# Plain-head v loads of five later batches issued from ScalarE's queue instead of SyncE's, in a fused sliding-attention and gated-unit kernel

## Chip, cores, metric

The kernel runs on one core of one Trainium2 chip. The metric is the device time in microseconds of one execution; lower is better. Three executions of the kernel before gave 179.93, 181.99 and 182.55 us, a median of 181.99 us. The profile shown below is of an execution of 178.74 us, in which the instructions span 176.8 us.

## What is computed

Eight batches, eight heads, 576 positions, head width 64. Heads 0 to 3 ("plain") attend to the last 32 positions, heads 4 to 7 ("dilated") to every fourth of the last 128. The attention output, 512 wide, goes through a gated linear unit with a causal convolution over five positions:

```python
scores = (q @ k^T) / 8, masked: plain  0 <= rel < 32;  dilated  0 <= rel < 128 and rel % 4 == 0
attn   = softmax(scores);  x = concat_heads(attn @ v)        # [8, 576, 512]
gate   = sigmoid(sum_k conv_w[k] * x shifted by 4 - k)
out    = (gate * (x @ w_val)) @ w_out                        # float32
```

All inputs and the output are float32 in main memory. The arithmetic on TensorE is bfloat16.

## The kernel before

The work is cut into 16 groups: group `g` is batch `g // 2`, with the plain heads where `g` is even and the dilated heads where it is odd. A group has two pairs of heads, and each pair is one step `i`, so there are 32 steps, four to a batch. A step computes scores (`scores`, L438), exponentials on ScalarE (L469), masks on VectorE (L478), the product with v (`attn_v`, L480) and the normalization (L517). In the same step stand, for earlier pairs, the convolution and its gate (`conv`, L569; the gate is ScalarE's L603), one to three value products (`val`, L606, each closed by L617 on VectorE), and output tiles (`out_tile`, L623: TensorE L628, ScalarE's copy `osb` L633, then one or two stores from L639). The next group is transposed meanwhile (`trans_main` L361 and `trans_rest` L408).

The order on each engine is the order in which the program states it: the kernel turns the scheduler off with `manual_schedule`, and the main loop (L734 to L803) writes out what each step holds. An engine takes its own instructions in that order.

Loads run three groups ahead. At the first pair of a group the loop calls `load_group(g + 3)` (L748), which issues the main parts of k and q (L122), the last 64 positions of k and q (`qk_rest`, L137 for plain groups and L142 for dilated ones), and then v. For a dilated group v is `v_st` and `vB_st` (L174 and L177). For a plain group v is two DMAs of L157, one for each half of the partitions of `vPst`, 64 partitions x 12 x 128 elements, 384 KB each; rows overlap between blocks, so 768 KB are moved. There are two `vPst` buffers, taken in turn by batches. `prep_v` (L197) casts them on GpSimd to the bfloat16 tile `vP`.

All these loads and all output stores are issued by SyncE, whose queue holds them in program order: at the beginning of a step it has k, q, rests and v of a later group, and at the end of a step the stores of a finished output tile. A store waits for ScalarE's `osb`. Only three small DMAs at the start go out from ScalarE. Every DMA adds 16 to one of eight completion semaphores, which SyncE's and ScalarE's DMAs share, and before it is issued its queue waits until the DMA that had that semaphore last has landed. So at most eight DMAs are under way at once, from both queues together. These eight are called lanes below[...].

Of the kernel before, what the change touches and what calls it, by code (L numbers as in the profile page):

```python
# [23 lines left out]
def kernel(  # L24
# [11 lines left out]
    nc = tc.nc  # L36
# [80 lines left out]
    def load_main(g, name, a, e, eng):  # L117
        src, h0 = (q if name == "q" else k), 4 * (g % 2)
        t = grp_tiles.setdefault(g, {})
        if name not in t:  # L120
            t[name] = qk_pool.tile([128, 4, DIL * D], FP32, name=f"{name}_nat")
        eng.dma_start(  # L122
            out=t[name][:, a:e, :],
            in_=src[g // 2, h0 + a:h0 + e, 0:RM, :].rearrange("h (p r) d -> p h (r d)", r=DIL))

    def load_rest(g, name, eng):


        src = k if name == "k" else q
        b, dil = g // 2, g % 2  # L130
        t = grp_tiles.setdefault(g, {})
        if "rest" not in t:
            t["rest"] = qk_pool.tile([128, 2, 2 * D], FP32, name="qk_rest")
        dst = t["rest"][:, 0 if name == "k" else 1, :]
        off = src.offset + ((b * H + 4 * dil) * S + RM) * D
        if not dil:
            eng.dma_start(  # L137
                out=dst.rearrange("p (h d) -> p h d", h=2),
                in_=bass.AP(tensor=src.tensor, offset=off,
                            ap=[[D, S - RM], [2 * S * D, 2], [S * D, 2], [1, D]]))  # L140
        else:
            eng.dma_start(  # L142
                out=dst,
                in_=bass.AP(tensor=src.tensor, offset=off,
                            ap=[[2 * D, 2 * TR], [S * D, 4], [1, 2 * D]]))

    def load_v_half(g, z, a, e, eng):


        b, per = g // 2, NB // 2  # L150
        first, dst = a * per, vPst[b % NVP]
        if b == 0 and a == 0 and z == 0:
            eng.dma_start(
                out=dst[16:D, 0, :],
                in_=v[0, 0, 0:96, :].rearrange("(p j) d -> p (j d)", j=2))
            first = 1
        eng.dma_start(  # L157
            out=dst[D * z:D * z + D, first:e * per, :],
            in_=bass.AP(
                tensor=v.tensor,  # L160
                offset=v.offset + (b * H * S + 192 * first + 96 * z - 32) * D,
                ap=[[2 * D, D], [192 * D, e * per - first], [1, 2 * D]]))

    def load_v(g, a=0, e=4, eng=nc.sync):
        b, dil = g // 2, g % 2
        t = grp_tiles.setdefault(g, {})
        if not dil:
            for z in range(2):
                load_v_half(g, z, a, e, eng)
        else:  # L170
            if "vst" not in t:
                t["vst"] = vst_pool.tile([128, 4, DIL * D], FP32, name="v_st")
                t["vBst"] = vst_pool.tile([128, 4, 2, D], FP32, name="vB_st")
            eng.dma_start(  # L174
                out=t["vst"][:, a:e, :],
                in_=v[b, 4 + a:4 + e, 0:RM, :].rearrange("h (p r) d -> p h (r d)", r=DIL))
            eng.dma_start(  # L177
                out=t["vBst"][:, a:e].rearrange("p h j d -> p h (j d)"),
                in_=v[b, 4 + a:4 + e, DIL * TB:S, :].rearrange("h (p j) d -> p h (j d)", j=2))

    def load_group(g):
        for name in ("k", "q"):
            load_main(g, name, 0, 4, nc.sync)
        for name in ("k", "q"):
            load_rest(g, name, nc.sync)
        load_v(g)

    def cast(g, name):

# [23 lines left out]
    def pair_info(i):  # L213
        b, c = i // NCH, i % NCH
        dil = int(c >= NCH // 2)
        return b, c, dil, 2 * b + dil, (c % 2) * 2
# [517 lines left out]
    for i in range(NP):  # L734
        b, c, dil, g, a = pair_info(i)

        if i == 0:
            load_weight(0, moe_w_val)
            load_pair(2, 0)
        elif i == 1:  # L740
            load_pair(2, 2)
        elif i == 2:
            load_weight(1, moe_w_out)
            load_pair(3, 0)
        elif i == 3:
            load_pair(3, 2)
            load_group(4)
        if c % 2 == 0 and 5 <= g + 3 < 2 * B:  # L748
            load_group(g + 3)
# [93 lines left out]
```

The softmax here doesn't subtract the row's maximum and nothing guards it: scores larger than these inputs give would overflow.

## Time and profile before

| | |
|---|---|
| device time, median of three | 181.99 us (179.93 to 182.55) |
| TensorE matmul busy | 159.5 us, 90% of the span |
| VectorE busy | 119.5 us, 68% |
| ScalarE busy | 113.8 us, 64% |
| GpSimd busy | 64.5 us, 36% |
| DMA traffic | 43.43 MB, 246 GB/s over the span |
| DMAs of L157 from SyncE, issue | 20 issues, 602 / 618 / 1896 ns (min, median, max) |
| DMAs of L157, issue to landing | 4.0 / 7.6 / 9.2 us |

A page of the profile has the busy time of each engine, the span cut in 40 slices with the busy share of each in tenths, the chain of work that ended last, the groups of instructions with their mean durations, and the DMA issues. "SPq" and "ACTq" are the issue queues of SyncE and ScalarE; the duration of an entry there is the time in which the queue is taken up by the DMA, the wait for its lane often included, and not the transfer. A timeline lists an engine's instructions in order of time: start, duration, engine, line, operation, and in square brackets how long the engine was idle before and what released it.

### The profile page before, as it was taken

The page shows a single profiled execution, that of the slowest core. Times are in us where ns is not written, and L with a number is a line of the kernel's source. Part 1 is how long each engine was busy: PE and PEld are TensorE (multiplying, and loading weights), DVE is VectorE, ACT ScalarE, POOL GpSimd, SP SyncE. Part 2 cuts the span into 40 slices and gives each one's busy share as a digit, 9 for nine tenths or more (in the row PEclk, how much of TensorE's full clock was granted, in tenths as well). Part 3 has the DMA queues.
Part 4 walks back from the last instruction along what each step waited for, and adds up shares of the span by engine and source line. Part 5 has one row for each costly group of instructions (what it writes and reads, how often), then busy time and mean ns, then how long its engine had stood idle before and what let it go on. Part 6 is the DMA issues. An engine that isn't in the chain of part 4 may idle for free.

```text
span 176.8 us, 6900 instructions
## 1 busy us (share of the span) xinstructions
PE 159.5 (90%) x2875; PEld 106.6 (60%) x2875; DVE 119.5 (68%) x299; ACT 113.8 (64%) x215; POOL 64.5 (36%) x129
## 2 busy tenths in 40 slices
PE   6798877989898899999997999789999999999990
PEld 2355544666576676677665667557677766665540
DVE  4397849773768776888695677577697869783320
ACT  3437835558777577778776777378867886654441
POOL 7673449659407610770085009300940500000000
PEclk9969999999999999999999999999999999999998
DMA  4999999999999999999999999999999322224344
GB/s 148 240 268 348 325 230 285 324 303 237 296 335 243 318 335 343 173 287 356 307 188 300 345 318 192 330 323 329 204 360 339 112 63 59 63 63 120 102 159 155
DMA packets 51528, 43.43 MB, mean 246 GB/s; under 512 B 6965, under 2 KB 45861, under 8 KB 51498
## 3 DMA queue, kind: packets, MB, share of 16 engines
q1 hardware_dynamic: 50944, 42.67, 89.1%
q8 instruction: 22, 0.36, 0.9%
q10 hardware_dynamic: 554, 0.34, 0.6%
q14 instruction: 8, 0.07, 0.1%
HBM read 33.56 MB, written 9.44 MB: 243 GB/s over the span
## 4 chain that ended last, share of the span: by engine, by line
PE 63%; DMA 21%; ACT 6%; DVE 5%; issue 2%; SPq 1%; ACTq 0%
PE ps_bank L628 16%; PE ps_bank L611 15%; PE ps_bank L594 10%; DMA out_dram<-osb 8%; PE ps_bank L378 5%; DMA qk_rest<-in_q_dram 4%; DMA k_nat<-in_k_dram 3%; DMA vPst<-in_v_dram 3%; PE ps_sc L499 3%; PE ps_sc L513 3%; PE ps_sc L449 3%; PE ps_bank L548 2%; DMA q_nat<-in_q_dram 2%; PE ps_sc L466 2%; DVE et L478 2%
## 5 line engine op out<-in xcount | busy, mean ns | idle before, releaser
L469 ACT ACTIVATE et<-ps_sc 128x576 bf16<-128x576 f32 x64 | 38.2, 649 | 13.7 <-PE ps_sc L449 9.0
L633 ACT ACTIVATE osb<-ps_bank 128x512 f32<-128x512 f32 x36 | 21.9, 609 | 28.9 <-PE ps_bank L628 18.0
L617 DVE SCALAR_TENSOR_TENSOR y<-gate,ps_bank 128x288 bf16<-128x288 bf16 x64 | 28.3, 450 | 13.0 <-PE ps_bank L611 10.6
L594 PE MATMUL ps_bank<-xT,conv_diag 64*64 64x288 bf16 (+1 forms) x768 | 27.6, 266 | 0.6 <-ACT osb L633 0.6
L529 DVE TENSOR_TENSOR xn<-ps_sc,rec 128x768 bf16<-128x768 f32 (+1 forms) x27 | 25.8, 955 | 0.9
L603 ACT ACTIVATE gate<-ps_bank 128x288 bf16<-128x288 f32 x64 | 23.1, 423 | 1.8 <-PE ps_bank L594 1.7
L478 DVE TENSOR_TENSOR et<-et,mask_d 128x576 bf16<-128x576 bf16 x32 | 15.8, 495 | 10.2 <-ACT et L469 10.2
L611 PE MATMUL ps_bank<-xT,w_val_s 128*128 128x288 bf16 x128 | 20.7, 285 | 2.1 <-issue 1.3
L193 POOL CAST k_b<-k_nat 128x512 bf16<-128x512 f32 x10 | 6.5, 681 | 42.3 <-DMA k_nat<-in_k_dram 33.1
L594 PEld LDWEIGHTS <-conv_diag 64*64 64x64 bf16 x768 | 18.9, 106 | 3.6 <-issue 1.2
L611 PE MATMUL ps_bank<-xT,w_val_b 128*128 128x288 bf16 x128 | 20.1, 286 | 0.4 <-DVE xT L563 0.4
L628 PEld LDWEIGHTS <-y 128*128 128x128 bf16 x144 | 12.6, 97 | 11.8 <-DVE y L617 0.9
L478 DVE TENSOR_TENSOR et<-et,mask_p 128x576 bf16<-128x576 bf16 x32 | 16.0, 501 | 4.8 <-ACT et L469 4.8
L202 POOL CAST vP<-vPst 128x768 bf16<-128x768 f32 x16 | 13.1, 841 | 15.6 <-DMA vPst<-in_v_dram 5.8
L628 PE MATMUL ps_bank<-w_out_s,y 128*128 128x512 bf16 x72 | 18.3, 379 | 0.1
L628 PE MATMUL ps_bank<-w_out_b,y 128*128 128x512 bf16 x72 | 18.5, 379 | 0.0
L563 DVE COPY xT<-ps_bank 128x576 bf16<-128x576 bf16 x32 | 14.6, 455 | 4.7 <-PE ps_bank L561 2.4
L611 PEld LDWEIGHTS <-w_val_s 128*128 128x128 bf16 x128 | 12.0, 97 | 6.2 <-issue 1.0
L207 POOL CAST vA<-v_st 128x512 bf16<-128x512 f32 x16 | 11.3, 705 | 10.3 <-DMA v_st<-in_v_dram 5.3
L611 PEld LDWEIGHTS <-w_val_b 128*128 128x128 bf16 x128 | 11.6, 98 | 3.7 <-issue 0.2
L393 ACT COPY kT<-ps_bank 128x1024 bf16<-128x1024 bf16 (+1 forms) x10 | 8.5, 849 | 6.1 <-PE ps_bank L370 5.9
L528 DVE RECIPROCAL rec<-ps_sc 128x12 f32<-128x12 f32 (+1 forms) x27 | 6.2, 231 | 7.7 <-PE ps_sc L499 6.7
(100 smaller groups left out, 248.4 us busy)
## 6 DMA issues: line engine op xcount, KB each, us to landing
k_nat<-in_k_dram SPq DMA_DIRECT2D x12, 512.0 KB, 6.0
q_nat<-in_q_dram SPq DMA_DIRECT2D x12, 512.0 KB, 6.9
vPst<-in_v_dram SPq DMA_DIRECT2D x12, 384.0 KB, 7.7
v_st<-in_v_dram SPq DMA_DIRECT2D x6, 512.0 KB, 5.7
k_nat<-in_k_dram SPq DMA_DIRECT2D x8, 256.0 KB, 5.9
out_dram<-osb SPq DMA_DIRECT2D x8, 256.0 KB, 6.1
q_nat<-in_q_dram SPq DMA_DIRECT2D x7, 256.0 KB, 5.8
out_dram<-osb SPq DMA_DIRECT2D x8, 224.0 KB, 5.4
```

Of the source, the lines that this page charges most:

```text
L202: nc.gpsimd.tensor_copy(vPs[b % NVP][:, a:e, :, 0:D], vPst[b % NVP][:, a * NB // 2:e * NB // 2, :].rearrange("p (h u) (j d) -> p h (u j) d ...
L207: nc.gpsimd.tensor_copy(vAs[b % NVD][:, a:e, :, 0:D], t["vst"][:, a:e, :].rearrange("p h (r d) -> p h r d", r=DIL))
L469: nc.scalar.activation(out=e3, in_=ps[:, :, 0:HB], func=AF.Exp, scale=scale)
L478: nc.vector.tensor_tensor(out=e3, in0=e3, in1=m, op=ALU.mult)
L529: nc.vector.tensor_tensor(out=dst, in0=av[:, :, :, 0:D], in1=rec[0:R, :, :, None].to_broadcast([R, 2, 6, D]), op=ALU.mult)
L563: nc.vector.tensor_copy(xTs[b % NXT][:, c, :, 2:], pr)
L594: nc.tensor.matmul(out=pss[G][D * hp:D * hp + D, o * T:(o + n) * T], lhsT=conv_diag[D * h:D * h + D, c, K - 1 - m, :], rhs=xt[D * h:D * h ...
L603: nc.scalar.activation(out=gate, in_=pss[G][:, 0:HB], func=AF.Tanh, scale=0.5)
L611: nc.tensor.matmul(out=ps[:, 0:HB], lhsT=w[:, mc, c * 128:(c + 1) * 128], rhs=xt[:, mc, 2 * G:2 * G + 2, 2:], start=(mc == 0), stop=(mc == ...
L617: nc.vector.scalar_tensor_tensor(out=y_half[G][:, c, b % YB * HB:(b % YB + 1) * HB], in0=gates.pop((b, c, G)), scalar=1.0, in1=ps[:, 0:HB] ...
L628: nc.tensor.matmul(out=ps, lhsT=y_half[G][:, c, y0:y0 + 128], rhs=w[:, c, :], start=(c == 0), stop=(c == NCH - 1),)
L633: nc.scalar.mul(out=osb, in_=ps, mul=0.5)
```

## The change

The two L157 DMAs of groups 6, 8, 10, 12 and 14 (plain heads of batches 3 to 7) are issued from ScalarE's queue. Their place in the program is the same, at the end of `load_group`, which the loop calls at the beginning of steps 6, 10, 14, 18 and 22. All other loads and all stores stay on SyncE. The change is for taking v out of SyncE's queue, where it stands behind the k and q loads of its group and ahead of the stores of the following output tiles.

```diff
         for name in ("k", "q"):
             load_rest(g, name, nc.sync)
-        load_v(g)
+        load_v(g, eng=nc.sync if g % 2 or g < 6 else nc.scalar)
```

In the program as built, TensorE, VectorE and GpSimd have the same instructions in the same order. ScalarE has five more places with two DMAs each, every one between the last instruction of the step before and the two exponentials (L469) of its own step; SyncE has these ten DMAs fewer.

## The prediction

> **What bounds the kernel now.** I read the page's busy rows and slices first, then the chain that ended last, the timelines of the three queues around steps 6, 10 and 14, and the waits. The slices:
>
> ```profile
> PE   6798877989898899999997999789999999999990
> ACT  3437835558777577778776777378867886654441
> DMA  4999999999999999999999999999999322224344
> ```
>
> From the fifteenth slice (62 us) on TensorE is full but for three slices, ScalarE has room, and the DMA engines are busy until 137 us. The chain of waits names TensorE for 63% of the span; from 31 us on each step goes scores, exponentials on ScalarE, mask, product with v, with other TensorE work filling the wait. A step that ScalarE enters late is therefore a step that TensorE ends late. Where ScalarE already loses time, the waits view says why (total, times, longest):
>
> ```profile
> ACT osb L633 <- DMA out_dram<-osb: 5.7, 3, 2.8
> SPq L142 <- DMA vPst<-in_v_dram: 4.1, 7, 1.7
> ```
>
> The first row: copies of output tiles wait for an earlier store to land, because SyncE runs late. The second: a small load waits for an unrelated v to land, because they share a lane. SyncE's timeline shows the lateness:
>
> ```profile
> 50.46 0.70 SPq L137 DMA_DIRECT2D qk_rest<-in_q_dram  x1
> 51.26 2.55 SPq L157 DMA_DIRECT2D vPst<-in_v_dram  x2
> 53.91 3.60 SPq L639 DMA_DIRECT2D out_dram<-osb  x4
> ...
> 59.68 0.58 SPq L142 DMA_DIRECT2D qk_rest<-in_k_dram  x1
> ...
> 75.07 0.40 SPq L122 DMA_DIRECT2D k_nat<-in_k_dram  x1
> ...
> 78.24 0.54 SPq L174 DMA_DIRECT2D v_st<-in_v_dram  x1
> ```
>
> and ScalarE's timeline the same stretch:
>
> ```profile
> 36.81 1.19 ACT L469 ACTIVATE et<-ps_sc 128x576 bf16<-128x576 f32 x2 [0.98 <-PE ps_sc L466]
> ...
> 54.24 1.01 ACT L400 COPY qA<-ps_bank 128x1024 bf16<-128x1024 bf16 x1
> 56.14 1.44 ACT L469 ACTIVATE et<-ps_sc 128x576 bf16<-128x576 f32 x2 [0.88 <-PE ps_sc L466]
> 57.66 0.71 ACT L603 ACTIVATE gate<-ps_bank 128x288 bf16<-128x288 f32 x2
> ...
> 61.29 0.60 ACT L633 ACTIVATE osb<-ps_bank 128x512 f32<-128x512 f32 x1 [1.75 <-DMA out_dram<-osb]
> ...
> 74.53 0.60 ACT L633 ACTIVATE osb<-ps_bank 128x512 f32<-128x512 f32 x1 [0.97 <-PE ps_bank L628]
> 75.21 1.19 ACT L469 ACTIVATE et<-ps_sc 128x576 bf16<-128x576 f32 x2
> ```
>
> The exponentials at 36.81, 56.14 and 75.21 are those of steps 6, 10 and 14. When ScalarE is at step 10, SyncE has still to issue the rest of k of group 7 (59.68), which step 8 states; when ScalarE is at step 14 (75.21), SyncE issues k of group 9 (75.07), which step 12 states. SyncE is some two steps behind.
>
> [...] with lanes taken the two v issues take 2.55 us, not 2 x 0.62. [...] The DMA row above leaves no idle engine to win. [...] The trace bounds the run-ahead: the semaphore instruction of step 14's first exponential lies at 74.6, just after `osb` starts at 74.53, and that of the second at 75.2. So ScalarE's queue looks ahead by one instruction, no more.
>
> **The change, part by part.** It removes ten issues from SyncE and puts them on ScalarE, with their waits. The transfers are the same bytes. The built program gives the wait for each: its lane's last user must have landed (the data waits, on casts of two batches earlier, are long met; the cast of batch 1's v runs at 30.49).
>
> ```
> step  6: v_st of group 3, first half; v_st of group 3, second half
> step 10: third store of the first output tiles; rest of k of group 7
> step 14: k of group 9;  v_st of group 9
> step 18: k of group 11; v_st of group 11
> step 22: k of group 13; v_st of group 13
> ```
>
> All are SyncE's DMAs, stated 1 to 2 steps before, in a queue that is some two steps late. Behind the waiting DMA on ScalarE stand the two exponentials of the step and two gates; VectorE's masks, the product with v, and the value product that needs the bank which the first gate frees wait for those.
>
> *Step 6.* The second half of v_st of group 3 has landed at 38.13, where GpSimd's cast (L207) starts after a 1.61 us wait for it. With an issue of 0.62 the exponentials start at 38.75 instead of 36.81 and end 1.19 later, at 39.94; mask 0.45, then the second product with v at 40.4 instead of 39.12: **+1.3 us**.
>
> *Step 10.* Rest of k of group 7 is issued at 59.68 and lands 5.4 us later (DMA view of that moment), at 65.1. In the changed kernel v of group 6 (51.26 to 53.81) no longer stands ahead of it in SyncE's queue: 2.65 us with the gap, so it lands at 62.4. The second v is issued by 63.0; two exponentials (1.19) and the first gate (0.42) end at 64.6. In the profile that gate ends at 58.1 and the value product that takes its bank starts at 58.27. So 6.3 late, of which 1.3 was there: **+5.0 us**. Bounds: if SyncE gains nothing, 65.1, +7.7; if SyncE could issue that rest already where the stores began (53.9), 59.3, +1.9. I take the middle case, since lanes still pace SyncE, while the moved v takes the bandwidth earlier instead of adding to it.
>
> *Steps 14, 18, 22.* ScalarE is now 6 us later and SyncE has caught up, until it waits for ScalarE's own `osb` of step 12, whose stores stand ahead of k of group 9. That `osb` ends at 66.03 in the profile (65.43 + 0.60). Then SyncE issues two stores, k, q, two rests and v_st at about 0.55 each: 3.9 us; v_st lands 5.4 after that, so 9.3 after `osb`, at 75.3 on the old clock. ScalarE reaches its first v at 74.55 and its second 0.62 later, at 75.2: a wait of 0.1 or so. The second issue ends at about 75.9 instead of the exponential's 75.21. The value product at 76.76 starts just when the first gate ends (76.29 + 0.42), so the delay goes through to TensorE: 0.7 to 0.9, taken as 0.8, three times: **+2.4 us**. Bounds: 0.5 (issue beside `osb`), and 2.4 if v_st takes the 7.0 us to landing that it took at 28.5.
>
> *What is given back.* With SyncE less late its stores land before the copies need their buffers. The 1.75 us wait at 61.29 holds a convolution bank: L594 goes on at 61.94 instead of 61.06, so 0.8. The exponentials of steps 21 and 22 are 6.19 us apart (108.42, 114.61), those of 17 and 18, the same kind, 4.52 (88.31, 92.83): 1.67. Steps 19 and 20: 4.39 against 4.23, 0.16. Together **-2.6 us**. SyncE's ten freed issues are worth nothing more: it waits for lanes and `osb`, and loads end at 137 us, long before the end.
>
> Sum: 1.3 + 5.0 + 2.4 - 2.6 = +6.1 us on 182.0: 188.1, forecast **188 us**, slower by 3.3%.
>
> **Rivals.**
> - *Recurring waits* (18%). SyncE does not catch up while ScalarE stands, since the DMA engines are full and the landings stay at 7 us: 7.7 at step 10 and 2.4 at each later one. 1.3 + 7.7 + 7.2 - 2.6 = +13.6: 195.6. For it: the DMA row. Against it: during a stand no new stores come up, and a stand of 6 us is room for 6 x 0.28 = 1.7 MB at the traced 280 to 300 GB/s.
> - *Issue cost alone* (17%). The lanes are free when ScalarE comes: five times 0.65 less 2.6, +0.6: 182.6, the same. Against it: landing times that the trace shows, 8 us after ScalarE's place at step 10.
> - *Not slower: a gain* (8%). Issues hide in ScalarE's idle 36%, lanes are free, and the store waits go: 182.0 - 2.6 = 179.4. For it: those waits are in the trace and SyncE is late. Against: the same as in the case before, and at step 14 `osb` and the exponentials follow without a gap.
>
> **How the numbers follow.** The forecast case has 57%, between 185 and 191.5 by the bounds of steps 10 and 14. The range reaches down over the case of issue cost to 183, and up to 195 into the recurring waits. Over 2% slower begins at 185.6: 0.57 and 0.18, less a small part of the forecast below it, 0.73. Within 2%: 0.22. Faster by over 2% needs under 178.4, beyond the gain case: 0.05.
>
> **What would show it.** Right: two ACTq entries of L157 before the exponentials of steps 6, 10, 14, 18 and 22; a gap on ScalarE of some 6 us between qA (L400) and step 10's exponentials, and TensorE idle there; gaps under 1.5 us at steps 14 to 22; `osb` waits for stores gone; SyncE's v_st of group 9 within 5 us of step 12's `osb`. Wrong: no gap at step 10, or gaps of 2 us and more at each of the later three, or exponentials that are late with TensorE busy all the same.

## The result, and the profile after

The changed kernel takes 196.01 us, the median of four runs (195.18 to 198.01), against 182.27 us for the kernel before (four runs, 179.93 to 183.55). The ratio is 1.082, with a 95% interval of 1.067 to 1.096: slower by 13.7 us. Run again beside the later experiments, the same kernel took 197.18 us, a ratio of 1.095 [1.088, 1.103]. A ratio compares the faster executions of each kernel, those within 1.5% of its fastest, so it can differ from the ratio of the two medians, in this document by up to 1.2 points (a point is 1% of the time of the kernel before). The direction was forecast; the size of 6.1 us was too small.

The traced execution of the changed kernel took 195.18 us with a span of 193.3, 16.5 us more than the traced span of before (176.8). The traces therefore show somewhat more than the medians. The slices of the page, with the granted TensorE clock (PEclk) added; a slice is 4.8 us. The second fence has the clock row of the kernel before:

```profile
PE   6789698869598239999999789996999999989990
ACT  3357645259445054775787378847777688743341
PEclk9889969999979856999999999999999999999998
DMA  5999999999999999397988998989979222122455
```

```profile
PEclk9969999999999999999999999999999999999998
```

Most of the loss is in one place. In the thirteenth to sixteenth slices (58 to 77 us) ScalarE's digits are 5, 0, 5, 4 and TensorE's 8, 2, 3, 9, and the granted clock goes 9, 8, 5, 6. Before, only the third slice was under 9 in that row, and the last. A smaller hole is in TensorE's row from the ninth to the eleventh slice (6, 9, 5), and the clock has a 7 in the twelfth. The 6 in the sixth slice of the clock row lies before the first moved DMA (35.89 us) and is no effect of the change. After 77 us the rows look like those of before. The chain that ended last can't be compared: in this profile it breaks off after accounting for 30% of the span.

The start of the first exponential of a step, from ScalarE's timelines, tells where the time goes. The last column is what was added since the row above:

| step | before | after | later by | added |
|---|---|---|---|---|
| 5 | 31.30 | 31.96 | 0.66 | 0.7 |
| 6 | 36.81 | 39.27 | 2.46 | 1.8 |
| 8 | 47.59 | 49.36 | 1.77 | -0.7 |
| 9 | 52.33 | 57.84 | 5.51 | **3.7** |
| 10 | 56.14 | 69.28 | 13.14 | **7.6** |
| 13 | 70.69 | 85.21 | 14.52 | 1.4 |
| 14 | 75.21 | 90.64 | 15.43 | 0.9 |
| 17 | 88.31 | 103.74 | 15.43 | 0 |
| 18 | 92.83 | 110.36 | 17.53 | 2.1 |
| 19 | 99.49 | 115.53 | 16.04 | -1.5 |
| 22 | 114.61 | 130.42 | 15.81 | -0.2 |
| 31 | 154.84 | 171.30 | 16.46 | 0.7 |

Two terms have to be read with care. The traced execution of before was one of the quicker of that kernel, and the -1.5 at step 19 is no effect of the change: the traces of all the kernels below show it (-1.4 or -1.5), also the one whose program is that of before up to step 22. It is a delay of that one execution of before.

ScalarE's timeline at the five places (start, duration, engine, line, operation, then the idle time before and its releaser):

```profile
35.89 0.65 ACTq L157 DMA_DIRECT2D vPst<-in_v_dram  x1
...
38.56 0.60 ACTq L157 DMA_DIRECT2D vPst<-in_v_dram  x1
39.27 1.19 ACT L469 ACTIVATE et<-ps_sc 128x576 bf16<-128x576 f32 x2 [2.45 <-DMA k_nat<-in_k_dram]
...
54.26 1.01 ACT L400 COPY kA<-ps_bank 128x1024 bf16<-128x1024 bf16 x1 [3.10 <-PE ps_bank L378]
...
59.76 1.01 ACT L400 COPY qA<-ps_bank 128x1024 bf16<-128x1024 bf16 x1
62.20 6.97 ACTq L157 DMA_DIRECT2D vPst<-in_v_dram  x2
69.28 1.19 ACT L469 ACTIVATE et<-ps_sc 128x576 bf16<-128x576 f32 x2 [8.51 <-DMA vPst<-in_v_dram]
...
89.14 1.40 ACTq L157 DMA_DIRECT2D vPst<-in_v_dram  x2
90.64 1.19 ACT L469 ACTIVATE et<-ps_sc 128x576 bf16<-128x576 f32 x2 [0.99 <-PE ps_bank L594]
...
107.66 2.59 ACTq L157 DMA_DIRECT2D vPst<-in_v_dram  x2
...
128.25 2.07 ACTq L157 DMA_DIRECT2D vPst<-in_v_dram  x2
```

At step 10 ScalarE has done its last copy at 60.77 and starts the exponentials at 69.28: it stands for 8.51 us. The profile names the v DMA, which is the last event before; what the queue waits for is the lane of that DMA, held by the rest of k of group 7. By the semaphore events of the trace the two have one semaphore: the rest of k goes out at 61.43 and lands at 68.49, and the second v goes out at 68.57. In the traces of both kernels the 181 DMAs of SyncE and ScalarE use eight completion semaphores, with 16 updates for each DMA on seven of them. In each trace the landing of the DMA before on the same semaphore is known for 150 DMAs; none of them goes out sooner than 0.016 us after it. All ten pairs of the prediction's list are in the events of the trace after. The rest of k is in SyncE's timeline:

```profile
55.98 2.98 SPq L639 DMA_DIRECT2D out_dram<-osb  x4
...
61.43 0.56 SPq L142 DMA_DIRECT2D qk_rest<-in_k_dram  x1
...
83.63 0.54 SPq L174 DMA_DIRECT2D v_st<-in_v_dram  x1
```

It takes 7.1 us to land (the DMA view of that moment). The second v is issued then, in 0.6 us, and ScalarE goes on. In the waits (total, times, longest) the product of values behind the first gate shows what this does to TensorE:

```profile
PE ps_bank L611 <- ACT gate L603: 11.3, 4, 7.0
...
POOL vP L202 <- DMA vPst<-in_v_dram: 10.5, 4, 6.7
...
ACT et L469 <- DMA vPst<-in_v_dram: 8.5, 1, 8.5
```

TensorE waits 7.0 us at one time for a gate that is behind the stand. The copies that waited 5.7 us for stores in the kernel before no longer do. The middle line is the other place, between steps 8 and 9: GpSimd's cast of v of group 4, before and after, from GpSimd's timelines:

```profile
46.70 1.59 POOL L202 CAST vP<-vPst 128x768 bf16<-128x768 f32 x2 [2.08 <-PE ps_bank L628]
```

```profile
51.76 1.59 POOL L202 CAST vP<-vPst 128x768 bf16<-128x768 f32 x2 [6.72 <-DMA vPst<-in_v_dram]
```

Before, the cast waits for TensorE, and its data are there. After, it waits for the data until 51.76. The v of group 6 now goes out at 35.89 and 38.56 instead of 51.26, in the middle of other loads. The DMA views of the moment give the two halves of v of group 4, issued from SyncE at 38 to 39 us, a median of 6.8 us to landing before and 11.5 after, and k of group 5 12.7 us after. ScalarE's `kA` copy at step 8 then waits 3.10 us for transposes (L378) of that k. After the hole TensorE does not run at its full clock (length of the window, then busy us and count of PE, PEld, DVE, ACT and POOL, granted clock, DMA share, GB/s):

```profile
46.00:56.00 10.00, 7.42 (x127) 4.73 (x122) 4.12 (x11) 6.05 (x13) 1.59 (x2) 0.83 1.15 271
```

The 0.83 is a mean: from 52.4 to 55.6 us the granted clock is 0.50. So the 3.7 us at step 9 are a wait for late loads and, behind it, a stretch at half clock.

### The profile page after: what moved, and what is told of

Read it like the earlier page. It is cut to its first block, busy times and chain, and to the rows that moved or that the text cites. A ratio compares the mean times of both kernels' runs of the same rounds, so it can differ in the third digit from the quotient of the medians.

```text
span 193.3 us, 6875 instructions
## 1 busy us (share of the span) xinstructions
PE 163.0 (84%) x2850; PEld 109.1 (56%) x2875; DVE 120.9 (63%) x299; ACT 114.2 (59%) x215; POOL 64.5 (33%) x129
## 3 DMA queue, kind: packets, MB, share of 16 engines
q10 hardware_dynamic: 8394, 4.27, 10.6%
## 5 line engine op out<-in xcount | busy, mean ns | idle before, releaser
L469 ACT ACTIVATE et<-ps_sc 128x576 bf16<-128x576 f32 x64 | 38.1, 648 | 29.3 <-PE ps_sc L449 10.2
L611 PE MATMUL ps_bank<-xT,w_val_s 128*128 128x288 bf16 x128 | 21.5, 295 | 11.9 <-ACT gate L603 11.3
L478 DVE TENSOR_TENSOR et<-et,mask_p 128x576 bf16<-128x576 bf16 x32 | 17.4, 543 | 4.7 <-ACT et L469 4.7
L207 POOL CAST vA<-v_st 128x512 bf16<-128x512 f32 x16 | 10.5, 658 | 11.3 <-DMA v_st<-in_v_dram 11.3
L400 ACT COPY kA<-ps_bank 128x1024 bf16<-128x1024 bf16 (+1 forms) x10 | 8.6, 858 | 6.4 <-PE ps_bank L378 6.2
```

Of the source, the lines that this page charges most:

```text
L207: nc.gpsimd.tensor_copy(vAs[b % NVD][:, a:e, :, 0:D], t["vst"][:, a:e, :].rearrange("p h (r d) -> p h r d", r=DIL))
L469: nc.scalar.activation(out=e3, in_=ps[:, :, 0:HB], func=AF.Exp, scale=scale)
L478: nc.vector.tensor_tensor(out=e3, in0=e3, in1=m, op=ALU.mult)
L611: nc.tensor.matmul(out=ps[:, 0:HB], lhsT=w[:, mc, c * 128:(c + 1) * 128], rhs=xt[:, mc, 2 * G:2 * G + 2, 2:], start=(mc == 0), stop=(mc == ...
```

## Experiments

All edits are against the kernel before unless it is said otherwise. Theory A in the expectations is the prediction's own mechanism; the other letters are explained in them.

**One place alone, first or last.** Only v of group 6 (step 6), and only v of group 14 (step 22):

```diff
-        load_v(g)
+        load_v(g, eng=nc.scalar if g == 6 else nc.sync)
```

> Group 6 alone has its two v DMAs on ScalarE's queue; groups 8 to 14 are as before. Theory A (a DMA on ScalarE waits for SyncE's backlog, and early v transfers make the loads ahead of them land later): step 6 costs its wait of about 2 us on ScalarE, and the loads of groups 4 and 5 land later, which costs about 3.5 us at step 8; no wait at step 10. 187 us, ratio 1.025 to 1.035. Theory B (only the issues and waits on ScalarE cost, not the transfers): +1.3 to 1.8, at most 184. Theory C (each of the five places costs the same share of the 14 us): +2.8, 185.

182.61 us against 181.76, ratio 0.997 [0.991, 1.003]. In the trace 2.8 us are added at step 6 and 1.9 between steps 8 and 9; then 0.7 come back at step 11 and 1.1 at step 22. The 1.1 does not come from v leaving SyncE's queue: from group 8 on this kernel has v on SyncE, as before. A's 1.025 to 1.035 was missed: this one v from ScalarE costs nothing that can be measured; its second DMA was let go when `v_st` of group 3 landed, as in the changed kernel (last event of that landing at 38.50, issue at 38.56), and no long stand follows. The run shows one thing more, in SyncE's timeline:

```profile
57.05 1.96 SPq L639 DMA_DIRECT2D out_dram<-osb  x4
...
62.22 0.56 SPq L142 DMA_DIRECT2D qk_rest<-in_k_dram  x1
```

The rest of k of group 7 goes out at 62.22, not earlier than in the kernel before (59.68), although no v stands ahead of it. How much later it is can't be told from two traces: in the runs below that have v of group 6 still on SyncE it goes out between 59.36 and 62.53. Why nothing is gained is read from the thin loads below.

> Group 14 alone on ScalarE's queue, at step 22. In the kernel before, v_st of group 13 is issued at 114.50 and lands 5.1 us later, at 119.6, when ScalarE has come to step 22 at 114.1. Theory D: ScalarE stands until 119.6, TensorE's clock falls for some us after it: 5 to 7 us, ratio 1.03 to 1.04. Theory C: one fifth of the loss, 2.8 us, ratio 1.015.

The same line with `g == 14`: 190.16 us, ratio 1.053 [1.044, 1.061]. This one place, the last, costs 1 to 1.6 us in the trace after; alone it costs more than half of what the five cost together. ScalarE's timeline, and the windows of the trace (stretch, length, busy us of PE, PEld, DVE, ACT and POOL, granted clock, DMA share, GB/s):

```profile
120.35 3.77 ACTq L157 DMA_DIRECT2D vPst<-in_v_dram  x2
124.22 1.19 ACT L469 ACTIVATE et<-ps_sc 128x576 bf16<-128x576 f32 x2 [5.55 <-DMA vB_st<-in_v_dram]
```

```profile
120.00:124.00 4.00, 0.00 (x0) 0.00 (x0) 0.00 (x0) 0.00 (x0) 0.00 (x0) 0.63 0.98 305
124.00:128.00 4.00, 2.24 (x20) 1.60 (x20) 2.03 (x6) 2.70 (x5) 0.00 (x0) 0.50 1.12 297
```

From 120 to 124 us nothing but DMA is busy, and the granted clock is down to a half afterwards. Step 22 loses 6.2 us and step 23, at half clock, 2.6. A debt would explain it: SyncE runs about two steps behind, and the first place whose lane is held by a late DMA pays for that lead. The forecast had 0.8 us for this place, and fails here; the debt theory had it at 1.03 to 1.04, and is too low. The place of group 6 pays no such debt: the DMA of group 3 that its second DMA waits for lands some 2 us after ScalarE gets there (36.53 to 38.50 in the trace after).

**The first place taken away.** From group 8 on, and from group 10 on:

```diff
-        load_v(g)
+        load_v(g, eng=nc.sync if g % 2 or g < 8 else nc.scalar)
```

> Groups 8 to 14 on ScalarE's queue, group 6 back on SyncE's. In the built program the second v of group 8 waits at step 10 for the first v of group 6, which SyncE issues at about 52.5 us in the kernel before and which takes about 8 us to land. Theory A: no loss at steps 6 to 9; ScalarE stands at step 10 until about 61 (5 us) and TensorE runs at a lower granted clock after it, then 1 to 2 us at each of steps 14, 18 and 22, less the store waits of 2 to 3 us: 188 to 190 us, ratio 1.03 to 1.045. Theory B: the same. Theory C: four fifths of the loss, 193.

194.69 us, ratio 1.066 [1.058, 1.074], above the interval that was expected. Step 10 loses 5.1 us, step 14 7.4 and step 15 2.2 more; the end of the trace lies 16.7 us later.

```profile
58.42 2.74 ACTq L157 DMA_DIRECT2D vPst<-in_v_dram  x2
61.26 1.19 ACT L469 ACTIVATE et<-ps_sc 128x576 bf16<-128x576 f32 x2 [5.97 <-DMA out_dram<-osb]
...
82.85 5.43 ACTq L157 DMA_DIRECT2D vPst<-in_v_dram  x2
88.38 1.19 ACT L469 ACTIVATE et<-ps_sc 128x576 bf16<-128x576 f32 x2 [7.44 <-DMA out_dram<-osb]
```

Here ScalarE stands twice, 5.97 and 7.44 us, where the changed kernel stands once. So the debt is not always paid at one place; why it comes up a second time here was not isolated.

> Groups 10, 12 and 14 alone on ScalarE's queue. Theory D (a debt: the first DMA on ScalarE makes it wait until SyncE's backlog is worked off, wherever that is, and the next one pays what is left): ScalarE stands at step 14 for about 8 us and for some more at step 18, in all nearly as much as with five groups: 12 to 16 us, ratio 1.06 to 1.08. Theory C (every place costs the same share): three fifths of the loss, 8.5 us, ratio 1.045.

With `g < 10`: 192.78 us, ratio 1.053 [1.040, 1.067], between the debt theory's 1.06 to 1.08 and the 1.045 of equal shares; the interval excludes neither. In the trace, of an execution of 194.18 us, the first long loss is now at step 14 (5.6 us and 2.3 at step 15), then 3.1 at step 18. Five, four, three places or the last alone give 1.082 to 1.095, 1.066, 1.053 and 1.053, and the place of group 6 alone 0.997. The loss does not go by the number of places, but by whether a place meets a SyncE DMA that is late.

**What the step from 8 to 9 owes to the moved v.** Since the programs are the same up to there, the traces can be sorted. Added between steps 8 and 9, with v of group 6 early from ScalarE: 3.7, 4.5, 1.9, 4.5 and 5.8 us (the changed kernel twice, this v alone, and the two kernels with idle products below), 4.1 in the mean. With that v in its old place on SyncE: 0 (before), 0 (from 8), 1.7 (from 10), 1.0 (only 14) and 2.9 (GpSimd from 8), 1.1 in the mean. The difference of 3 us is what the move costs there, roughly, for the two sets overlap. Part of it is the clock: the four traces with 3.7 to 5.8 us, and the one with 2.9, have 3 to 7 us at a granted clock of 0.50 between 49 and 59 us; the one with v of group 6 alone has none, and 1.9 us. The wait and the half clock behind it were not separated by a run.

**The data or the waits.** One kernel leaves the loads of v of groups 6 to 14 out. The other is the changed kernel with its ten DMAs moving one block of twelve each:

```diff
-        load_v(g)
+        g % 2 == 0 and g >= 6 or load_v(g)
```

> The v loads of groups 6, 8, 10, 12 and 14 are left out altogether (v of batches 0 to 2 is used again in later batches, so the output of batches 3 to 7 differs), which bounds what any other queue could bring. Theory A: TensorE sets the pace, so 3.9 MB less traffic and ten issues less bring only the store waits back: 2 to 4 us, 178 to 180, ratio 0.98 to 0.99. Rival T: the DMA engines set the pace up to 137 us, and 3.9 MB less at about 280 GB/s bring up to 14 us: 168 to 172.

177.14 us, ratio 0.970 [0.964, 0.976]: somewhat more gain than A's 0.98 to 0.99, and far less than the rival's 168 to 172 us.

```diff
-        load_v(g)
+        load_v(g, eng=nc.sync if g % 2 or g < 6 else nc.scalar)
...
+        last = e * per if g < 6 else 1
-            out=dst[D * z:D * z + D, first:e * per, :],
+            out=dst[D * z:D * z + D, first:last, :],
```

> The ten DMAs stay on ScalarE's queue, but each moves one of its twelve blocks (32 KB instead of 384 KB), so the waits on ScalarE remain and nearly all of the v transfers are gone; most of v of batches 3 to 7 is not loaded and the output of these batches differs. The built program gives other partners for some waits: at step 10 the third and fourth store of the first output tiles, which should land at about 60, at steps 14, 18 and 22 k and the rest of k. Compared with leaving these loads out altogether (0.970): theory A (waiting on ScalarE for SyncE's backlog is what costs): a stand of 4 to 5 us at step 10, about 0.7 at each later place: ratio 1.00 to 1.02. Rival T (the v transfers beside the other loads are what costs): no more than the issues, 0.97 to 0.98.

182.47 us, ratio 1.011 [1.005, 1.016], as A expected. ScalarE's queue with its ten waits and hardly any bytes costs 4.1 points over no loads at all (1.011 less 0.970; 3.3 by the medians, and 3.4 us between the two traces). Step 10 is 3.3 us later than without loads, and the later places some 0.6 us each. Between steps 8 and 9 only 0.1 us is added: what the changed kernel loses there comes from the bytes. The two kernels differ in one thing more: the thin one waits at step 10 for two stores, and not for the rest of k of group 7, so its stand is not the same wait without the bytes. The stand at step 10:

```profile
57.30 1.89 ACTq L158 DMA_DIRECT2D vPst<-in_v_dram  x2
59.30 1.19 ACT L470 ACTIVATE et<-ps_sc 128x576 bf16<-128x576 f32 x2 [4.00 <-DMA k_nat<-in_k_dram]
```

SyncE's timeline of the thin kernel is the one on which the forecast rests:

```profile
44.26 0.54 SPq L175 DMA_DIRECT2D v_st<-in_v_dram  x1
...
45.91 2.48 SPq L122 DMA_DIRECT2D k_nat<-in_k_dram  x1
...
57.06 0.56 SPq L142 DMA_DIRECT2D qk_rest<-in_k_dram  x1
```

Beside the same three issues in the other kernels' timelines:

| issued by SyncE at | v_st of group 5 | k of group 6 | rest of k of group 7 |
|---|---|---|---|
| before | 44.03 | 45.75 | 59.68 |
| no v from group 6 on | 44.93 | 46.95 | 57.57 |
| changed, thin | 44.26 | 45.91 | 57.06 |
| changed | 48.58 | 50.85 | 61.43 |
| changed, second trace | 48.27 | 51.34 | 61.59 |
| only v of group 6 | 48.78 | 50.63 | 62.22 |

With almost no bytes in v, SyncE keeps the times of before up to k of group 6 and then gains 2.6 us, as forecast. With the bytes it is late at k of group 6 already: 50.6 to 52.6 us in the five traces that have this v early on ScalarE, against 45.75 to 47.8 in six that have it on SyncE, so 3 to 5 us. SyncE's issues wait for landings, and the landings are later while the early v is under way: in the trace after k of group 5 goes out at 40.34, after a landing on its semaphore at 40.27, and its rest at 45.56, when the first half of the early v has landed at 45.54, also on its semaphore; v of group 4 took 11.5 us to land instead of 6.8. So the queue out of which v was taken is slowed by that same v.

The loads cost 3.0 points from SyncE (1.000 less 0.970), their issues included; their bytes cost 7.1 from ScalarE (1.082 less 1.011, or 8.4 with the second measurement). The traces give a reason for more than half of that: the stand at step 10 ends when a DMA of SyncE lands, and with the bytes under way that is at 68.5 us, in the thin kernel before 59.3. How the 7.1 points divide was not measured.

**Another queue with no such waits.** The early place, from GpSimd, to whose DMAs the built program gives completion semaphores of their own. From 36 to 100 us of its trace their issues take 1.49 to 1.69 us for two, and none stands for a landing:

```diff
-        load_v(g)
+        load_v(g, eng=nc.sync if g % 2 or g < 6 else nc.gpsimd)
```

> The same ten v DMAs, at the same places of the program, from GpSimd's queue. In the built program they use completion semaphores of their own and wait for nothing but GpSimd's casts, so ScalarE has no new wait, and the transfers are as early as in the changed kernel or earlier. Theory A: the stand at step 10 is gone; what remains is the later landing at step 8, 3 to 4 us, less store waits of 2 to 3 us: 182 to 186 us, ratio 1.00 to 1.02. Rival T (the transfers themselves, earlier and beside k and q, are what costs): as slow as the changed kernel, 192 or more.

187.63 us, ratio 1.027 [1.019, 1.036], over A's 1.00 to 1.02 and far under the rival's 192 us. With no lane wait and nothing added to ScalarE's queue, about a third of the loss of the changed kernel remains. Most of it is lost between steps 8 and 9, 6.8 us in this trace, which has a granted clock of 0.50 from 55.1 to 61.8 us behind the wait. The cast of v of group 4 on GpSimd:

```profile
55.16 1.71 POOL L202 CAST vP<-vPst 128x768 bf16<-128x768 f32 x2 [7.33 <-DMA vPst<-in_v_dram]
```

and the median of the DMA issues (KB each, us to landing), 5.7 before:

```profile
v_st<-in_v_dram SPq DMA_DIRECT2D x6, 512.0 KB, 10.6
```

So loads of SyncE can land later for v from a second queue alone. Not all do: k landed in 5.6 us here against 6.0 before (medians of twelve). From group 8 on, the same edit with `g < 8`:

> Plain v of groups 8 to 14 from GpSimd's queue (semaphores of its own, no wait on ScalarE), group 6 on SyncE's. Theory A with early transfers as a second cost: without group 6's early transfer the loss of 1.027 shrinks, and the store waits come back: ratio 0.99 to 1.01. If the early transfers of the later groups cost as much as group 6's: 1.02 to 1.03.

187.90 us, ratio 1.044 [1.039, 1.049], over both expectations. Leaving the first place out doesn't help: now steps 17 and 18 lose 3.4 and 2.7 us. (It also loses 2.9 at step 9 and 2.1 at step 20. The first is before its first changed load, and the run with v of group 14 alone shows 2.2 at step 20 as well, before its own: such delays come and go from one execution to the next.) GpSimd waits for k in five places:

```profile
POOL k_b L193 <- DMA k_nat<-in_k_dram: 54.4, 5, 13.0
```

**The place or the queue.** The same v at the end of the following step, behind the stores of its output tiles, from each of the three queues:

```diff
-        load_v(g)
+        if g % 2 or g < 6:
+            load_v(g)
...
+        if c == 3 and 6 <= g + 3 < 2 * B:
+            load_v(g + 3)
```

> All v stays on SyncE's queue; the plain v of groups 6 to 14 is issued at the end of the step after (steps 7, 11, 15, 19, 23), behind the stores of the output tiles that it stood ahead of. If those stores' lateness (the waits of osb for a store, 5.7 us in all) is what v in SyncE's queue costs, this brings back 1 to 2.6 us without any wait on ScalarE: ratio 0.985 to 0.995. Against it: v then lands 5 us later, and GpSimd's cast waits for it; if that is late for the product with v, 1.00 or more.

179.65 us, ratio 0.992 [0.987, 0.996] against the kernel before. This is faster than both kernels, than the one before by under 1%. The waits that GpSimd has for v are long, and stop nobody who is needed:

```profile
POOL vP L203 <- DMA vPst<-in_v_dram: 26.7, 10, 4.6
...
ACT osb L634 <- DMA out_dram<-osb: 2.9, 1, 2.9
```

The waits of `osb` for stores are 2.9 us instead of 5.7, which fits stores that are no longer behind v. It doesn't prove it: the run with v of group 6 alone on ScalarE has 2.9 as well, with four later v still ahead of the stores.

> The ten DMAs on ScalarE's queue, at the end of steps 7, 11, 15, 19 and 23 instead of the beginning of 6, 10, 14, 18 and 22; compared with 0.9915 for the same place on SyncE's queue. In the built program each still waits for a DMA that SyncE's queue got one to two steps before: at the end of step 11 for the second rest of group 8, which the kernel before issues at about 67.1 and lands some 5 us later, at about 72, when ScalarE is there at about 65. Theory A (the waits on ScalarE are the larger part): a stand of about 7 us at the end of step 11, half clock after it, smaller ones later: ratio 1.05 to 1.08. Theory T (the early place is what costs): 0.99 to 1.01.

The same with `load_v(g + 3, eng=nc.scalar)`: 190.66 us, ratio 1.064 [1.052, 1.076].

```profile
47.90 4.54 ACTq L157 DMA_DIRECT2D vPst<-in_v_dram  x2
52.54 1.19 ACT L470 ACTIVATE et<-ps_sc 128x576 bf16<-128x576 f32 x2 [4.18 <-DMA qk_rest<-in_k_dram]
```

The ratio lies in the expected range, the places were others: a stand of 7 us was expected at the end of step 11. ScalarE stands at the end of step 7, and again at the end of step 11 (3.75 us): 4.2 and 3.5 us are added there.

> The ten DMAs on GpSimd's queue, at the same later place. If the early place was what the runs on GpSimd's queue paid for (1.027 and 1.044): ratio 0.985 to 1.00, as on SyncE's queue. If issuing from GpSimd, or a second stream beside SyncE's, costs by itself: 1.02 to 1.04 again.

With `eng=nc.gpsimd`: 184.54 us, ratio 1.026 [1.011, 1.041]. In one table, each entry the ratio to the kernel before:

| v of groups 6 to 14 from | beginning of the step | end of the next step |
|---|---|---|
| SyncE | 1 | 0.992 |
| GpSimd (no shared lanes) | 1.027 | 1.026 |
| ScalarE (shared lanes) | 1.082 and 1.095 | 1.064 |

The intervals of the two ratios from GpSimd reach from 1.011 to 1.041, so these may be under 2%. The queue makes more of a difference than the place: ScalarE against GpSimd, that is, the waits in the queue of an engine that is needed, is worth 3.7 to 6.8 points, the place 1.8 to 3.1 from ScalarE and next to nothing from GpSimd. GpSimd against SyncE is 2.7 to 3.5. But the columns are places in the program and not times. From GpSimd v of group 6 goes out early at the later place too; the first line is that kernel's, the second that of the same place on SyncE:

```profile
47.25 1.69 POOL L157 DMA_DIRECT2D vPst<-in_v_dram  x2
```

```profile
55.39 1.93 SPq L157 DMA_DIRECT2D vPst<-in_v_dram  x2
```

SyncE's queue sent it at 51.26 in the kernel before. So all four kernels of the two lower rows send this v earlier than SyncE does, and the theory that sending it early is what hurts is not refuted for the 2.7 to 3.5 points. What of them is the early time, what a second stream beside SyncE's order, and what GpSimd's own time for issuing (0.75 to 0.94 us each, with its casts behind), stays open.

**The clock after the stand.** The changed kernel with idle products added, whose result nobody reads, in a part of a bank that is free:

```diff
+        if (b, c) == (2, 0):
+            for _ in range(60):
+                nc.tensor.matmul(out=pss[1][:, HB:512], lhsT=junk[:, 0:128], rhs=junk[:, 0:512 - HB],
+                                 start=True, stop=True, skip_group_check=True)
```

> The changed kernel with 64 small matmuls on TensorE (128 x 128 by 224 columns, into columns of the second convolution bank that nothing reads) after the convolution of step 10, where TensorE stood idle for 7.0 us; nothing waits for them. If the lower granted clock after the stand (0.50 from 70 to 76 us) is a cost of its own, the clock stays near 1.0 there and steps 10 to 12 take about 2.5 us less than in the changed kernel: ratio 1.065 to 1.07 against 1.082. If the clock costs nothing, since other things set the pace there, or if the small matmuls come in the way: 1.08 or more.

With 64 products and `(2, 1)`: 204.25 us, ratio 1.120 [1.107, 1.132]. They came a step too late, after the stand, and 6.4 us are added there, about 0.1 each. The run says nothing on the clock.

> As the run before with small matmuls, whose 64 matmuls turned out to follow the convolution of step 11 instead, after the stand; here 60 of them, at the 0.103 us each that run showed, follow the convolution of step 10 itself and fill about 6.2 of the 7.0 us in which TensorE stood. If the halved granted clock after the stand is a cost of its own, steps 10 to 12 take 2 to 3 us less than in the changed kernel, which is timed beside it: ratio lower by 0.010 to 0.015. If the pace there is set by something else, the same ratio as the changed kernel; if the matmuls are in the way, higher.

> The changed kernel once more, beside the other three, for a direct comparison: 1.075 to 1.09.

With `(2, 0)` the 60 products lie within the stand. The median is 194.0 us beside 197.18 of the changed kernel (its ratio of 1.095 is a little over the 1.075 to 1.09 that was expected); the six runs spread from 189.76 to 196.73, so no ratio is given and the trace carries the reading. Its windows, then those of the changed kernel measured beside it:

```profile
66.00:70.00 4.00, 4.00 (x45) 4.00 (x43) 0.00 (x0) 0.00 (x0) 0.45 (x1) 1.00 1.15 183
...
73.00:76.00 3.00, 2.95 (x55) 2.11 (x57) 2.48 (x8) 1.99 (x4) 0.00 (x0) 1.00 1.13 223
```

```profile
66.00:70.00 4.00, 0.00 (x0) 0.00 (x0) 0.00 (x0) 0.00 (x0) 0.00 (x0) 0.59 1.11 228
...
73.00:76.00 3.00, 2.78 (x21) 1.70 (x20) 2.10 (x6) 0.37 (x2) 0.00 (x0) 0.50 1.14 192
```

ScalarE stands in both (no ACT from 66 to 70), but with the products TensorE stays busy and its clock at 1.00. From 73 to 76 us it then does 55 products instead of 21. From the first exponential of step 10 to that of step 12 it takes 8.55 us instead of 10.90 (11.15 in the profile after): the half clock costs some 2.4 us, on top of the stand, by one trace of each; the medians, 3.2 us apart, point the same way. The thin loads agree: with a stand of 4 us, in which TensorE is idle for 2.5 us and its clock stays at 1.00, step 11 there gains 1.3 us, as it does in the kernel with busy products (1.3), while in the two traces of the changed kernel it loses 0.9 and 1.0.

## Why the prediction failed, step by step

The direction and the main mechanism were right: ScalarE's queue waits for SyncE's unlanded DMAs through shared lanes, most of all at step 10, and the exponentials behind it are late. What was to be seen was seen: two L157 entries before the exponentials of the five steps, a gap between `qA` and step 10's exponentials, an idle TensorE, no `osb` wait for a store, and `v_st` of group 9 issued 3.3 us after step 12's `osb` (80.32 to 83.63). Of the gaps under 1.5 us at steps 14 to 22 only the first came (0.99; then 2.18 and 1.66). The size was wrong. Term by term:

- **Step 6, forecast +1.3.** Measured +1.8, and 1.2 to 3.2 in the other four traces that have this place: the right kind, a little small.
- **Step 10, forecast +5.0. This is the step that failed**: "v of group 6 (51.26 to 53.81) no longer stands ahead of it in SyncE's queue: 2.65 us with the gap, so it lands at 62.4". The rest of k of group 7 landed at 68.5. It was issued at 61.43 and not at 57.0, and took 7.1 us instead of 5.4. Taking v out of SyncE's queue gained nothing: this rest goes out at 61.43 to 62.63 in the five traces with v of group 6 early on ScalarE, and at 59.36 to 62.53 in six that have it on SyncE. The gain exists if v moves almost no bytes: 57.06 in the thin kernel. With the bytes SyncE falls 3 to 5 us behind up to k of group 6, which takes the gain back. In the table step 10 adds 7.6 us (7.6 to 8.2 in four traces). The forecast's 5.0 counts more than that, all lateness at step 10 beyond that of step 6; so counted the trace has 10.7 (13.14 less 2.46), over the 7.7 that the forecast named as its upper bound.
- **Between steps 8 and 9, forecast nothing, measured +3.7.** Of the same step the forecast said "the moved v takes the bandwidth earlier instead of adding to it", as if bandwidth taken earlier cost nothing. The v of group 4 and k of group 5, which were needed sooner, landed later: 11.5 us instead of 6.8, and 12.7. Sorted over ten traces the move is worth about 3 us there; with thin loads it is worth nothing, and from GpSimd, without any lane wait, 6.8. The hole that the late loads leave is followed by 3.2 us at half clock in the trace after, for which the forecast had no term.
- **After the stand, forecast -0.8 at step 11, measured +1.4 over steps 11 to 13.** The `osb` wait did go; step 11 gains 1.3 us in the two traces where TensorE's clock stays up, at 1.00, after a stand, and 0.2 to 0.7 in eight of the nine kernels without one at step 10. But TensorE ran at half clock for some 5 us after the stand. That is 2.4 us by the run that kept TensorE busy, and had no term.
- **Steps 14, 18 and 22, forecast +0.8 each.** 0.9, 2.1 and about 1.6, if the 1.67 that was to come back at step 22 did, as it does without v (1.7): 4.6 in place of 2.4. The second trace has 1.6, 0.8 and, reckoned in the same way, 3.5, with another 1.7 at step 23. At step 14 the working held almost to the digit: the partner was to land 9.3 us after step 12's `osb`, and landed after 9.6 (83.63 + 6.3 - 80.32).
- **Given back, forecast -2.6.** The 1.67 at step 22 does come back without v, but 1.1 of it also comes back with v of group 6 alone moved, where nothing near step 22 was changed: most of it may be a delay of the one execution that was read. The 0.8 at step 11 was drowned by the clock. The -1.5 at step 19, which the forecast had not counted, is a delay in the one execution that was read, and nothing the change gave back. One trace of before was taken for the kernel's steady state.

The sum of the measured terms is 0.7 + 1.1 + 3.7 + 7.6 + 1.4 + 0.9 + 2.1 - 1.5 - 0.2 + 0.7 = 16.5 us in the traces. Of the 10.4 us by which they exceed the forecast, 6.3 lie between steps 8 and 10 (3.7, and 7.6 less 5.0). Apart from the clock they go back mostly to one assumption: that a transfer which moves 13 to 15 us forward in a full DMA system delays nothing.

The nearest rival was recurring waits, at 195.6 us. Its number is within 0.4 us of the result, but that is in part luck. That SyncE gains nothing at step 10 was right; its 7.7 there is too low by 3 us on its own count, since the rest of k landed at 68.5 and not at 65.1. Its 7.2 at the later places was 4.6 in the trace after and 5.9 in the second (7.6 with step 23). The late loads at step 8 and the clock are not in its sum. The rival of issue cost alone (182.6) is refuted by the trace: the lane was not free, and ScalarE stood for 8.51 us. The thin kernel's median of 182.47 us is the rival's number by chance; ScalarE stands for 4.00 us in it. The rival of a gain fails for ScalarE's queue; but the gain that it counted on, copies that no longer wait for stores, is in the trace, and may be what the later place on SyncE collects with its 0.992.

## To carry to other kernels

Before a DMA is moved to another engine's queue, write down what its issue will wait for there (completion semaphores that both queues share count: ScalarE stood 8.51 us for one here), and what is in order behind it; an engine on the path that sets the end should not be made to wait for a queue that runs late. When the DMA engines are full, expect a load that is moved earlier to take its time from loads that are needed sooner (11.5 us to landing instead of 6.8 for v of group 4 here); v from GpSimd, for whose lane nobody waited, cost 1.026 to 1.044, GpSimd's own issuing included. If the aim is to get stores out from behind a load, try the load later in the same queue first (0.992 here). And count the clock: a stand of TensorE can cost more than its own length (here 7.0 us, and some 2.4 us of half clock behind it).

## What the runs showed of the hardware that was not expected

- TensorE's last product before the stand ends at 63.8 us and the next begins at 70.82. Its granted clock was 0.50 from 66.0 on, 2.2 us into the stand, and stayed there until 76.2, some 5 us after work began again. In the run with v of group 14 alone it fell after 1.4 us of idle time (119.6 to 121.0). Holes of about 2 us went both ways: at step 9 one of 2.15 us was followed by half clock, in the thin kernel one of 2.51 us was not (mean granted clock of that whole trace 0.983, of the trace after 0.944). On the way back TensorE was not busy without breaks: for 2.2 of the first 3 us and 2.8 of the next 3:

```profile
66.00:70.00 4.00, 0.00 (x0) 0.00 (x0) 0.04 (x1) 0.72 (x2) 0.00 (x0) 0.50 1.19 179
70.00:73.00 3.00, 2.18 (x19) 1.57 (x19) 1.94 (x6) 1.98 (x4) 0.00 (x0) 0.50 1.11 338
73.00:76.00 3.00, 2.78 (x19) 1.36 (x18) 1.77 (x5) 0.73 (x2) 0.00 (x0) 0.50 1.15 264
76.00:80.00 4.00, 3.95 (x65) 2.88 (x62) 3.01 (x6) 2.96 (x6) 3.23 (x6) 0.97 0.62 159
```

- The same windows have the DMA share above 1 in the stand (1.19) while only 179 GB/s are moved. A full DMA row does not mean the same number of bytes at every time: 338 GB/s follow in the next window. The room in a stand that the forecast counted on, 6 us or 1.7 MB, was nearly there all the same, since the first part of the stand moved more: 249 GB/s from 62.5 to 68.5 us, 1.5 MB.
- The median time to landing of the 512 KB `v_st` went from 5.7 us to 10.6 when v came from GpSimd's queue at the early place, and to 6.9 at the later place, with nearly the same loss (1.027 and 1.026). So the late landing of `v_st` can't be the whole reason of the loss from GpSimd's queue.
